# Running the MLP tiles of one batch between the attention heads of the next, with the weights loaded at the start

## The chip, the cores and the metric

One core of a Trainium2 chip runs one launch that computes eight batches of attention and then an MLP over their output. The metric is the device time of a launch in microseconds (us). The time is the median of the runs.

The engines have short names: PE is TensorE, which does matmuls and transposes (PEld is its loading of weights), ACT is ScalarE, DVE VectorE, POOL GpSimd and SP SyncE. Tiles lie in SBUF, the working memory; matmuls write to PSUM, which is dealt out here in eight banks. PEclk is the clock that was granted to PE, as a share of full speed.

## The reference, cut to what matters

```python
def rmsnorm(x, g):
    rms = np.sqrt(np.mean(x * x, axis=-1, keepdims=True) + 1e-06)
    return x / rms * g
# q, k, v: (8 batches, 12 heads, 448, 64) float32
q_n, k_n = rmsnorm(q, g_q), rmsnorm(k, g_k)
attn = softmax(q_n @ k_n.T / sqrt(64))
x = (attn @ v) laid out as (3584 tokens, 768)
h = x @ w_in                     # (768, 2048)
g = 0.5 * h * (1 + tanh(sqrt(2/pi) * (h + 0.044715 * h**3)))
out = g @ w_out                  # (2048, 768), float32
```

The kernels put h * sigmoid(1.702 h) for the gelu. A batch makes 448 tokens; the MLP works in tiles of 512, so tile t needs batches up to (t + 1) * 512 / 448.

## The kernel before

It is two loops, one after the other. The first does a batch at a time: load and square q and k (POOL), sum (DVE), Ln and Exp for the inverse root (ACT), normalise (DVE), transpose on PE; then all 48 score matmuls with their exps, then all 48 PV matmuls; the result goes to a scratch `x` in DRAM.

```python
ps_t = pool("ps_t", bufs=2, PSUM); ps_s = pool("ps_s", bufs=3, PSUM); ps_o = pool("ps_o", bufs=2, PSUM)
for b in range(B):
    qTb = rmsnorm_T(q[b]); kTb = rmsnorm_T(k[b], extra_scale=gqk)
    vaug = vp.tile(...)                       # vp: 2 buffers
    nc.gpsimd.dma_start(vaug[:, :, :, 1:], v[b] ...)
    for h in range(H):
        for sk in range(4):
            scp = ps_s.tile(...); matmul(scp, kT, qT)
            nc.scalar.activation(exs[:, h, sk, :], scp, AF.Exp, scale=scale)
    for h in range(H):
        oap = ps_o.tile(...)                  # 4 PV matmuls accumulate
        osb = copy(oap); otp = transpose(osb) # otp shares ps_t
        xout = otp / its first column
    nc.sync.dma_start(x[b * S:(b + 1) * S, :], xout)
```

Then the attention's pools are closed; the weights are loaded as float32 and cast on ACT; `x` is read back transposed; and the MLP runs seven tiles.

```python
actx.close()
win = load_bf16(moe_w_in); wout = load_bf16(moe_w_out)   # 6 MB DMA each, then a cast on ACT
for c in range(6): nc.sync.dma_start_transpose(xTs[:, c, :], x[:, c * 128:(c + 1) * 128])
for t in range(7):
    for f in range(16):
        hps = ps_h.tile(...)                  # 2 banks; 6 matmuls
        sig = activation(hps, AF.Sigmoid, scale=1.702)
        gsb[:, f, :] = hps * sig
    for (dm0, dmsz) in ((0, 512), (512, 256)):
        for ts in range(4):
            op = ps_m.tile(...)               # 4 banks; 16 matmuls
            osb = copy(op); dma out
```

In the profiles `scp` is a score matmul, `oap` a PV matmul, `otp` the transpose back, `tp` the seven transposes of q or k, `hps` the first and `ops_t` the second MLP matmul.

## Time and profile before

| | before |
|---|---|
| median time | 778.9 us (776.3 to 784.1, 16 runs) |
| span of the profiled run | 776.8 us |
| PE / ACT / DVE / POOL busy | 599.5 / 368.9 / 291.4 / 138.8 us |
| attention, hole, MLP | 373.8, 62.7, 298.8 us |

The windows view of the kernel before, for its attention and the hole after it. The columns are the stretch, its length, then busy time and instruction count of PE, PEld, DVE, ACT and POOL, the granted clock of PE, the DMA share and the GB/s:

```profile
41.50:415.30 373.80, 292.17 (x1763) 163.37 (x1761) 193.39 (x309) 246.88 (x526) 111.78 (x39) 0.90 0.61 73
415.30:478.00 62.70, 6.09 (x12) 1.55 (x13) 0.56 (x1) 23.23 (x5) 0.00 (x0) 0.50 0.95 298
```

By their differences PE is idle for 81.6 us of the attention and 56.6 us of the hole, and for 4 us of the 298.8 us of MLP (busy 294.5). So some 138 us of PE time lie open, while the MLP alone has 294.5 us of PE work that needs only one finished batch to begin. That is what the change goes for.

### The profile page before, as it was taken

The page shows a single profiled execution, that of the slowest core. Times are in us where ns is not written, and L with a number is a line of the kernel's source. Part 1 is how long each engine was busy: PE and PEld are TensorE (multiplying, and loading weights), DVE is VectorE, ACT ScalarE, POOL GpSimd, SP SyncE. Part 2 cuts the span into 40 slices and gives each one's busy share as a digit, 9 for nine tenths or more (in the row PEclk, how much of TensorE's full clock was granted, in tenths as well). Part 3 has the DMA queues.
Part 4 walks back from the last instruction along what each step waited for, and adds up shares of the span by engine and source line. Part 5 has one row for each costly group of instructions (what it writes and reads, how often), then busy time and mean ns, then how long its engine had stood idle before and what let it go on. Part 6 is the DMA issues. An engine that isn't in the chain of part 4 may idle for free.

```text
span 776.8 us, 8528 instructions
## 1 busy us (share of the span) xinstructions
PE 599.5 (77%) x3392; PEld 323.3 (42%) x3392; DVE 291.4 (38%) x435; ACT 368.9 (47%) x705; POOL 138.8 (18%) x54
## 2 busy tenths in 40 slices
PE   0277788787877777877983105999999999999998
PEld 0152644435344353543531001464645445464645
DVE  1843765637456373652612001404041312223140
ACT  1169395582955829468581515324232323323231
POOL 7450631614316053150000000000000000000000
PEclk9879797978999999999997555999999999999999
DMA  6920922909229091390106994020201011010102
GB/s 150 133 72 4 211 72 71 143 1 147 66 82 133 0 165 49 104 40 0 37 1 262 241 370 96 7 75 1 75 7 62 22 41 41 28 54 15 68 1 81
DMA packets 101415, 62.67 MB, mean 81 GB/s; under 512 B 66304, under 2 KB 94976, under 8 KB 100608
## 3 DMA queue, kind: packets, MB, share of 16 engines
q0 software_dynamic: 43136, 5.51, 25.2%
q1 hardware_dynamic: 58240, 56.63, 24.0%
q8 instruction: 26, 0.43, 0.2%
q14 instruction: 13, 0.11, 0.0%
HBM read 45.61 MB, written 16.52 MB: 80 GB/s over the span
## 4 chain that ended last, share of the span: by engine, by line
PE 50%; ACT 23%; POOL 7%; DVE 7%; DMA 5%; SPq 5%; issue 4%; POOLq 0%; ACTq 0%
PE ops_t L192 19%; PE hps L177 18%; ACT exs L118 17%; PE oap L122 8%; POOL sq L72 5%; SPq L163 4%; DVE ss L74 3%; DMA x<-xout 2%; PE otp L130 2%; DMA raw<-in_q_dram 2%; PE tp L87 2%; DVE nrm L81 2%; ACT L78 1%; POOL vaug L104 1%; ACT osb L127 1%
## 5 line engine op out<-in xcount | busy, mean ns | idle before, releaser
L177 PE MATMUL hps<-xTs,dst 128*128 128x512 bf16 x672 | 163.2, 387 | 58.2 <-ACT dst L156 28.1
L118 ACT ACTIVATE exs<-scp 112x448 bf16<-112x448 f32 x384 | 170.7, 669 | 76.5 <-PE scp L115 76.0
L186 DVE TENSOR_TENSOR gsb<-hps,sig 128x512 bf16<-128x512 f32 x112 | 77.4, 692 | 262.8 <-ACT sig L185 262.8
L192 PE MATMUL ops_t<-dst,gsb 128*128 128x256 bf16 (+1 forms) x896 | 154.8, 326 | 0.0
L115 PE MATMUL scp<-xT_sb 128*112 128x448 bf16 x384 | 135.9, 366 | 24.4 <-ACT exs L118 2.3
L177 PEld LDWEIGHTS <-dst 128*128 128x128 bf16 x672 | 66.1, 99 | 145.2 <-issue 47.3
L87 PE MATMUL tp<-ident,nrm 128*128 128x128 bf16 x672 | 63.7, 249 | 65.3 <-DVE nrm L81 34.6
L192 PEld LDWEIGHTS <-gsb 128*128 128x128 bf16 x896 | 87.7, 98 | 59.6 <-DVE gsb L186 1.1
L185 ACT ACTIVATE sig<-hps 128x512 bf16<-128x512 f32 x112 | 66.8, 597 | 96.3 <-PE hps L177 76.6
L122 PE MATMUL oap<-exs,vaug 112*65 112x448 bf16 x384 | 111.9, 405 | 0.0
L115 PEld LDWEIGHTS <-xT_sb 128*112 128x112 bf16 x384 | 50.5, 135 | 85.3 <-issue 79.9
L87 PEld LDWEIGHTS <-nrm 128*128 128x128 bf16 x672 | 52.5, 113 | 79.1 <-issue 75.3
L72 POOL TENSOR_TENSOR sq<-raw 128x2688 f32<-128x2688 f32 x16 | 82.6, 5164 | 9.2 <-DMA raw<-in_q_dram 9.2
L200 ACT COPY osb<-ops_t 128x512 f32<-128x512 f32 (+1 forms) x56 | 26.8, 479 | 107.1 <-PE ops_t L192 107.1
L127 ACT CAST osb<-oap 65x448 bf16<-65x448 f32 x96 | 50.6, 560 | 43.8 <-PE oap L122 43.8
L74 DVE TENSOR_REDUCE ss<-sq 128x42 f32<-128x2688 f32 x16 | 47.2, 2951 | 61.6 <-POOL sq L72 61.6
L81 DVE TENSOR_TENSOR nrm<-raw,rinv 128x2688 bf16<-128x2688 f32 x16 | 53.0, 3314 | 18.4 <-ACT rinv L78 18.4
L130 PE MATMUL otp<-ident,osb 65*112 65x65 bf16 x384 | 37.8, 225 | 26.0 <-ACT osb L127 24.8
L134 DVE RECIPROCAL recip<-otp 112x4 f32<-112x4 bf16 x96 | 17.5, 182 | 106.0 <-PE otp L130 102.8
L130 PEld LDWEIGHTS <-osb 65*112 65x112 bf16 x384 | 33.7, 143 | 51.9 <-ACT osb L127 40.3
L122 PEld LDWEIGHTS <-vaug 112*65 112x65 bf16 x384 | 42.3, 126 | 28.8 <-issue 14.9
L80 POOL MEMSET nrm<- 128x2688 bf16 x16 | 37.4, 2337 | 52.6 <-PE tp L87 52.6
(21 smaller groups left out, 179.8 us busy)
## 6 DMA issues: line engine op xcount, KB each, us to landing
out_dram<-osb SPq DMA_DIRECT2D x28, 256.0 KB, 2.0
tmp<-in_moe_w_in_dram SPq DMA_DIRECT2D x1, 6144.0 KB, 18.0
tmp<-in_moe_w_out_dram SPq DMA_DIRECT2D x1, 6144.0 KB, 18.0
vaug<-in_v_dram POOLq DMA_DIRECT2D x8, 672.0 KB, 13.8
x<-xout SPq DMA_DIRECT2D x8, 672.0 KB, 4.2
out_dram<-osb SPq DMA_DIRECT2D x28, 128.0 KB, 1.7
raw<-in_q_dram SPq DMA_DIRECT2D x8, 0.2 KB, 9.4
raw<-in_k_dram SPq DMA_DIRECT2D x8, 0.2 KB, 6.9
```

Of the source, the lines that this page charges most:

```text
L72: nc.gpsimd.tensor_mul(sq, raw, raw)
L74: nc.vector.reduce_sum(ss, sq, axis=mybir.AxisListType.X)
L81: nc.vector.tensor_mul(nrm[:, :, :D], raw, rinv.to_broadcast([128, NC, D]))
L87: nc.tensor.transpose(tp[:, t * 128:(t + 1) * 128], nrm[:, g * 7 + t, :], ident)
L115: nc.tensor.matmul(scp, kT[:, sk * ST:(sk + 1) * ST], qT, start=True, stop=True)
L118: nc.scalar.activation(exs[:, h, sk, :], scp, AF.Exp, scale=scale)
L122: nc.tensor.matmul(oap, vaug[:, h, sk, :], exs[:, h, sk, :], start=(sk == 0), stop=(sk == nst - 1))
L130: nc.tensor.transpose(otp[:, si, :D + 1], osb[:, si * ST:(si + 1) * ST], ident[:D + 1, :D + 1])
L177: nc.tensor.matmul(hps, win[:, c, f * 128:(f + 1) * 128], xTs[:, c, t * NT:(t + 1) * NT], start=(c == 0), stop=(c == kc - 1),)
L185: nc.scalar.activation(sig, hps, AF.Sigmoid, scale=1.702)
L186: nc.vector.tensor_mul(gsb[:, f, :], hps, sig)
L192: nc.tensor.matmul(op, gsb[:, f, ts * 128:(ts + 1) * 128], wout[:, f, dm0:dm0 + dmsz], start=(f == 0), stop=(f == nf - 1),)
```

## The change

The intent is that an MLP tile runs as soon as its tokens are there, its matmuls filling PE's gaps in the attention of the next batch. Four things make that possible: both weights come early, cast by the DMA; all pools live to the end, and eight PSUM banks are split anew (`tp`/`otp` 1, `sc` 2, `oap` 2, `hps` 1, `ops` 2); sigmoid becomes tanh (sigmoid(a) is (1 + tanh(a/2))/2), so that gelu and exp need no different tables; and V, `xout` and `sq` shrink, and the exps are kept four tiles at a time instead of a whole batch, so that all fits SBUF. The order on each engine comes from the tool's scheduler, not straight from the text.

```diff
+    def load_weights():
+        nc.gpsimd.dma_start(win, moe_w_in ...)      # bf16 tiles: the DMA casts
+        nc.gpsimd.dma_start(wout, moe_w_out ...)
-    vp bufs=2; outp bufs=8; xp bufs=2
+    vp bufs=1; outp bufs=6; xp bufs=1
-        sq = stp.tile([128, NC, D], F32, tag="sq")
+        sq = stp.tile([128, NC, D], BF16, tag="sq")
-            tp = ps_t.tile(...)                     # 2 buffers
+            tp = psum.tile(..., tag="tp", bufs=1)
...
         for h in range(H):
+            oap = psum.tile([D + 1, S], F32, tag="oap", bufs=2)
             for sk in range(nst):
-                scp = ps_s.tile(...)                # 3 buffers
+                scp = psum.tile(..., tag="sc", bufs=2)
                 ... exp ...
+                nc.tensor.matmul(oap, vaug[:, h, sk, :], ex, ...)
-        (second loop over the heads with the PV matmuls)
...
+    def moe_tile(t):
+        xTt: six dma_start_transpose of x's 512 rows
         for f in range(nf):
-            hps = ps_h.tile([128, NT], F32, tag="h")          # 2 buffers
+            if t >= ntt - 2 and f % 3:
+                hps = psum.tile([128, NT], F32, tag="sc", bufs=2)
+            else:
+                hps = psum.tile([128, NT], F32, tag="hps", bufs=1)
-            nc.scalar.activation(sig, hps, AF.Sigmoid, scale=1.702)
-            nc.vector.tensor_mul(gsb[:, f, :], hps, sig)
+            nc.scalar.activation(sig, hps, AF.Tanh, scale=0.851)
+            nc.vector.scalar_tensor_tensor(gsb[:, f, :], sig, 1.0, hps, op0=ALU.add, op1=ALU.mult)
...
-                nc.scalar.copy(osb[:, :dmsz], op)
+                nc.scalar.mul(osb[:, :dmsz], op, 0.5)
...
+    attn_batch(0)
+    win, wout = load_weights()
+    for b in range(1, B):
+        attn_batch(b)
+        (every moe_tile whose tokens are complete before batch b)
+    (the remaining moe_tiles)
```

## The prediction

> **What bounds the kernel now.** I read the page first (slices and groups), then the chain that ended last, then stretches of the windows view, then the timeline. The kernel is two stages one after the other with a hole between them. The slices show it (40 slices of 19.4 us):
>
> ```profile
> PE   0277788787877777877983105999999999999998
> ACT  1169395582955829468581515324232323323231
> PEclk9879797978999999999997555999999999999999
> ```
>
> PE is at 7 to 8 tenths through the attention (slices 2 to 20), near nothing in three slices, and full to the end. The windows view puts numbers on one steady attention batch, the hole, and the second stage:
>
> ```profile
> core 0: us, PE busy (x) PEld busy (x) DVE busy (x) ACT busy (x) POOL busy (x), PEclk, DMA share, GB/s
> 219.30:267.10 47.80, 36.30 (x228) 20.31 (x228) 25.97 (x40) 30.57 (x67) 17.29 (x6) 0.93 0.77 88
> 416.00:478.00 62.00, 6.09 (x12) 1.55 (x13) 0.56 (x1) 23.23 (x5) 0.00 (x0) 0.50 0.95 299
> 560.00:776.00 216.00, 212.81 (x1144) 111.21 (x1142) 55.35 (x80) 67.69 (x122) 0.00 (x0) 1.00 0.11 39
> ```
>
> A batch takes 47.8 us with no engine full; the hole is 62 us with PE at half clock; the MLP is PE-bound at full clock. The chain of waits shows why a batch is 47.8 and not ACT's 31:
>
> ```profile
> 215.50 0.72 ACT osb L127 x2
> 216.24 1.28 ACT L76
> ...
> 230.53 2.03 POOL vaug L104
> 232.56 2.13 issue
> ...
> 237.01 5.70 POOL sq L72
> 242.73 2.95 DVE ss L74
> 245.69 0.60 DVE xT_sb L93
> 247.11 16.17 ACT exs L118 x37
> ```
>
> The last PV matmul frees a V buffer, POOL refills it and only then squares the next batch, DVE sums it, and the transposes and exps wait behind that in order. In the hole, the timeline has the weight loads and two casts on ACT (`ACT dst` 10.4 us each) and six DMA transposes; all 12.6 MB of weights move only when nothing else runs.
>
> The rows I cost with:
>
> ```profile
> L118 ACT ACTIVATE exs<-scp 112x448 bf16<-112x448 f32 x384 | 170.7, 669 | 76.5 <-PE scp L115 76.0
> L115 PE MATMUL scp<-xT_sb 128*112 128x448 bf16 x384 | 135.9, 366 | 24.4 <-ACT exs L118 2.3
> L186 DVE TENSOR_TENSOR gsb<-hps,sig 128x512 bf16<-128x512 f32 x112 | 77.4, 692 | 262.8 <-ACT sig L185 262.8
> ```
>
> **What the Trainium skill says.** "ScalarE: Activation LUTs", section Table sets: tanh is in the set of exp, sigmoid is in another. So tanh among exps needs no switch, and a sigmoid would. The order of the built program agrees: no table load stands before any tanh. The same page, section What ACT_TABLE_LOAD costs, gives about 1283 ns for a load; the trace has 1283 ns for each of its 23. "VectorE: DVE Perf Modes", section on the perf-mode tiers, has tensor_reduce at one element a cycle for either type, so the bf16 `sq` should not shorten the 2.95 us sum (no run here shows it yet). "TensorE: Matmul & The Clock Gate", section The HAM clock gate: an idle PE drops to half clock. The trace agrees: 0.50 in the hole, 1.00 in dense stretches.
>
> **The change part by part.** The instruction counts on PE are the same before and after (3,392 matmuls); they move. The order of the built program shows: batches 0 and 1 almost alone; tile 0 inside batch 2, tiles 1 to 4 inside batches 3 to 6; tile 5 has its few first matmuls inside batch 7 and nearly all of the rest after it, since most of its `hps` now want the `sc` buffers behind the attention; tile 6 last.
>
> PE's streaming cost, from dense stretches of the timeline and chain: scp and oap 0.19 us, transposes 0.107 (7 in 0.75), otp 0.087 (4 in 0.35), hps 0.216, ops_t 0.216 at 512 columns and 0.109 at 256. Counting the built order from the first score of a batch to that of the next gives PE floors of 31.5 (batch 0), 32.8 (1), 55.8 (2), 71.4 (3), 73.1 (4, 5, 6) and 126.5 us (7 with the tail): 543 us with the start's 6. That is the bound that nothing here can beat; the rest is what stalls in between.
>
> 1. *The hole* (62 us) goes. The weights come by casting DMA from POOL at the start, and each tile's transposes are issued some 50 us before their use in the order. The two casts (20.9 us of ACT) go too.
>
> 2. *Batches 0 and 1 get slower.* The transposes and `otp` share one PSUM buffer instead of two, so seven transposes and their copy no longer overlap: 0.9 (cold PE) + 0.04 + 0.65 + 0.04 = 1.65 us a group. Eight groups, one `ss` (2.95) and one `nrm` (2.95) stand before the first score: 19 us, against 8.6 before. The score buffers fall from 3 to 2 and PV is interleaved: a buffer's loop is exp 0.54, semaphore 0.05, one oap 0.19, score with latency 0.35, 0.04: 1.17 us for two exps, 0.585 each, where 37 exps in 16.17 us were 0.437. Twelve heads with their `osb` copy come to about 2.6 us each, 31 us; two split Ln/Exp pairs cost 2.5 us each (32 table loads against 23), the remaining transposes and DVE waits about 3. So batch 1 is 19 + 31 + 5 + 3 = 58 us against 47.8. Batch 0: first score at about 46 (the q and k copies on one buffer), plus 4 because the V load stands behind the 6 MB weight load on POOL's queue; then 31 + 5 + 6 of late batch-1 loads = 42, to 92.
>
> 3. *Batch 2 with tile 0's first part.* 19 us of transposes, 12 heads at about 3 us with some 60 MLP matmuls in the gaps, 7 of stalls: 62, to 212. Then the middle block, 8 groups of six hps, two ops_t, seven transposes. `hps` has one buffer; the chain before shows its loop directly at each tile's start: 1.31 PE + 0.02 + 0.61 ACT + 0.03 + 0.70 DVE + 0.04 = 2.71 us. The other PE work in it fills 1.18 of the 1.4 us wait. 8 x 2.71 = 21.7, plus one `nrm` on DVE in the way, 2.5: 24, to 236.
>
> 4. *Four steady segments* (batches 3 to 6). Two hps groups and the first scores, 6; 96 ops_t, 14.2 (PE-bound, ACT starves); 23 pairs of exps at 0.76 scp/oap + 0.18 otp + 0.43 MLP = 1.37 us of PE against the 1.17 loop, 31.5; Ln and table loads 2.5, `ss` and order misses 3; middle block 24. Sum 81, against a floor of 73; 4 x 81 = 324, to 560.
>
> 5. *The end.* 20 (tile 4's rest), 12 heads at 2.6 = 31, transition 1, then tiles 5 and 6 alone: 178 hps x 0.216 + 126 x 0.216 + 128 x 0.109 = 79.6, and 3.4 us to the end as before: 135. Total 695 us.
>
> The single V buffer (16.5 us from last oap to landed: 0.3 + 0.4 + 2.05 + 13.8) fits behind the 19 to 24 us of transposes, so I charge nothing. `scalar_tensor_tensor` for `tensor_mul` (one PSUM and one SBUF operand, 692 ns) and the halved output copy I take as equal.
>
> **The rivals.** (a) *PE-bound*: the gaps fill so well that the segments sit at 73 to 75 us and batches 0 and 1 at 48: 646 us. For it: MLP matmuls are independent of exps, and PE runs at clock 1.00 when dense. Against: every engine takes its instructions in a fixed order, and `hps`, `tp` and `otp` have one buffer each. (b) *ACT/DVE latency takes PE's place*: with single buffers each misplaced `ss`, `nrm` or Ln holds DVE or ACT for 3 us and with it PE; two per segment more than I charge, and segments of 90, give 735. For it: the before shows exactly such order misses (62 us of DVE waiting for POOL `sq`). (c) *The weight load starves the start*: 6 MB of casting DMA ahead of V, at the V load's own pace (0.67 MB in 13.8 us) instead of the plain loads' 18 us, would shift all by 20 to 40 us: 715 to 735. Against: rows of 8 KB against V's 256 B. (d) *The attention's losses eat the 62 us hole's gain*: 10 us in each of eight batches would be 80; but from batch 3 on the transposes lie beside MLP work, so it's 3 batches.
>
> **Range and chances.** 695, with (a) below and (b) or (c) above: 650 to 740 eight times in ten. The 2% border is 764; only (b) with (c) reach it. Faster 0.93, within 2% 0.05, slower 0.02.
>
> **What would show it.** Right: no stretch of PE below two tenths after slice 3; ACT `dst` rows gone; exps at 0.58 to 0.6 us each in batches 0 and 1; hps groups 2.7 us apart in the middle block; last two tiles at 42 us each; segments of 78 to 84 us; clock near 1.00 from batch 2 on. Wrong: the first score after 55 us (c); waits of PE for DVE copies or `gsb` over 60 us in the steady segments (b); PE over 95% busy there (a); or an `oap` held by the V load, which I took as hidden.

## The result, and the profile after

The changed kernel takes 682.5 us (median of 8 runs, 680.2 to 686.0) against 778.9 us: the ratio is 0.876, with a 95% interval of 0.874 to 0.878. Ratios here are the mean time of one kernel's runs over that of the other's runs of the same rounds, so not quite the ratio of the medians. The predicted 695 us was 12.5 us too slow; the result lies inside the range of 650 to 740. All outputs are right.

The slices of the changed kernel (40 slices of 17 us each):

```profile
PE   0265838766788799878998799888999799999998
...
ACT  0228846851885249824696256933396246942331
...
PEclk9997968776999999999999999999999999999999
```

The empty slices are gone: past the third, no slice of PE is below three tenths. The clock row shows where PE still idles enough to lose its clock: slices 4 to 10, which is where batches 0 and 1 lie.

The windows view of the changed kernel, cut from the first score of one batch to that of the next (batches 0 to 6), then the rest (columns as above). Batches 0, 1, 4 and 6 are shown; the cuts are 39.8, 102.4, 165.0, 232.9, 310.2, 389.4, 468.5 and 543.9 us:

```profile
39.80:102.40 62.60, 39.88 (x231) 23.15 (x230) 34.70 (x43) 41.32 (x76) 26.04 (x9) 0.82 0.96 141
102.40:165.00 62.60, 43.27 (x237) 24.88 (x236) 26.41 (x40) 35.18 (x69) 17.41 (x6) 0.75 0.67 81
...
310.20:389.40 79.20, 70.60 (x456) 40.16 (x453) 36.44 (x56) 46.72 (x92) 16.36 (x6) 1.00 0.63 83
...
468.50:543.90 75.40, 70.24 (x455) 39.98 (x453) 27.65 (x53) 40.66 (x84) 4.63 (x3) 1.00 0.47 51
```

Batches 0 and 1, nearly without MLP work, take 62.6 us each where the kernel before took 47.8. The segments of batches 4 and 5 are 79 us with PE busy for 70.6 of it: a whole MLP tile and a batch of attention. In the kernel before the two together cost 47.8 and a seventh of 298.8, which is 90.5 us, and the hole besides.

The chain that ended last, of the changed kernel, in the middle block between the heads of batch 2 and those of batch 3 (start, us, what):

```profile
212.58 1.42 PE hps L166 x6
214.02 0.61 ACT sig L171
214.65 0.70 DVE gsb L172
215.39 1.47 PE hps L166 x6
```

Six `hps` matmuls, their tanh, their multiply, and only then the next six: the one `hps` bank makes this a loop of 2.81 to 2.86 us. The transposes of the next batch and two `ops_t` matmuls lie in it.

The groups of the changed kernel that answer to the three shown of before (busy us, mean ns, and idle time before):

```profile
L130 ACT ACTIVATE ex<-scp 112x448 bf16<-112x448 f32 x384 | 191.3, 543 | 54.3 <-PE scp L126 52.6
...
L126 PE MATMUL scp<-xT_sb 128*112 128x448 bf16 x384 | 137.1, 370 | 0.0
L172 DVE SCALAR_TENSOR_TENSOR gsb<-sig,hps 128x512 bf16<-128x512 bf16 x112 | 76.8, 686 | 121.7 <-ACT sig L171 121.6
```

The exps are 543 ns each instead of 669. The difference is no gain in speed: in the kernel before exps stood back to back and their recorded times overlap. The new multiply costs the same as the old one, 686 against 692 ns.

### The profile page after: what moved, and what is told of

Read it like the earlier page. It is cut to its first block, busy times and chain, and to the rows that moved or that the text cites. A ratio compares the mean times of both kernels' runs of the same rounds, so it can differ in the third digit from the quotient of the medians.

```text
span 678.5 us, 8823 instructions
## 1 busy us (share of the span) xinstructions
PE 555.7 (82%) x3392; PEld 314.1 (46%) x3392; DVE 283.4 (42%) x435; ACT 365.8 (54%) x712; POOL 135.9 (20%) x56
## 4 chain that ended last, share of the span: by engine, by line
PE 56%; ACT 17%; DVE 10%; issue 9%; DMA 5%; POOL 4%; SPq 0%; ACTq 0%; POOLq 0%
PE hps L166 19%; PE ops_t L178 18%; ACT ex L130 9%; PE oap L131 8%; PE scp L126 6%; DVE gsb L172 5%; ACT sig L171 4%; DMA vaug<-in_v_dram 4%; PE tp L98 2%; DVE nrm L93 2%; POOL sq L84 2%; PE otp L138 2%; ACT osb L135 2%; ACT L130 1%; DMA raw<-in_q_dram 1%
## 5 line engine op out<-in xcount | busy, mean ns | idle before, releaser
L130 ACT ACTIVATE ex<-scp 112x448 bf16<-112x448 f32 x384 | 191.3, 543 | 54.3 <-PE scp L126 52.6
L166 PE MATMUL hps<-xTt,win 128*128 128x512 bf16 x672 | 178.4, 382 | 33.8 <-DVE gsb L172 29.3
L131 PE MATMUL oap<-ex,vaug 112*65 112x448 bf16 x384 | 138.5, 365 | 32.9 <-ACT ex L130 27.4
L178 PE MATMUL ops_t<-wout,gsb 128*128 128x256 bf16 (+1 forms) x896 | 161.2, 326 | 0.1
L172 DVE SCALAR_TENSOR_TENSOR gsb<-sig,hps 128x512 bf16<-128x512 bf16 x112 | 76.8, 686 | 121.7 <-ACT sig L171 121.6
L166 PEld LDWEIGHTS <-win 128*128 128x128 bf16 x672 | 66.2, 99 | 97.7 <-issue 42.6
L84 POOL TENSOR_TENSOR sq<-raw 128x2688 bf16<-128x2688 f32 x16 | 77.5, 4846 | 99.8 <-DMA raw<-in_q_dram 56.6
L185 ACT ACTIVATE osb<-ops_t 128x512 f32<-128x512 f32 (+1 forms) x56 | 26.9, 491 | 76.8 <-PE ops_t L178 76.8
L104 DVE TENSOR_SCALAR xT_sb<-tp,gqk 128x896 bf16<-128x896 bf16 x48 | 32.7, 682 | 79.6 <-PE tp L98 79.6
L86 DVE TENSOR_REDUCE ss<-sq 128x42 f32<-128x2688 bf16 x16 | 47.2, 2947 | 27.1 <-POOL sq L84 27.1
L93 DVE TENSOR_TENSOR nrm<-raw,rinv 128x2688 bf16<-128x2688 f32 x16 | 47.8, 2989 | 4.6 <-ACT rinv L90 4.6
## 6 DMA issues: line engine op xcount, KB each, us to landing
vaug<-in_v_dram POOLq DMA_DIRECT2D x8, 672.0 KB, 14.1
win<-in_moe_w_in_dram POOLq DMA_DIRECT2D x1, 3072.0 KB, 18.9
wout<-in_moe_w_out_dram POOLq DMA_DIRECT2D x1, 3072.0 KB, 41.1
```

What stands on the lines that cost most here:

```text
L84: nc.gpsimd.tensor_mul(sq, raw, raw)
L86: nc.vector.reduce_sum(ss, sq, axis=mybir.AxisListType.X)
L93: nc.vector.tensor_mul(nrm[:, :, :D], raw, rinv.to_broadcast([128, NC, D]))
L130: nc.scalar.activation(ex, scp, AF.Exp, scale=scale)
L131: nc.tensor.matmul(oap, vaug[:, h, sk, :], ex, start=(sk == 0), stop=(sk == nst - 1))
L166: nc.tensor.matmul(hps, win[:, c, f * 128:(f + 1) * 128], xTt[:, c, :], start=(c == 0), stop=(c == kc - 1),)
```

## The experiments

Each run was timed beside the kernel before on the same chip, and the ratios below are to it; the changed kernel's ratio is 0.876. One profile of each was taken. The changed kernel's own runs spread over 6 us, so differences of a few us between single profiles are read with care and the timed ratios decide.

### 1. Only the early weights, without the interleaving

The kernel before, with the two stages still apart. `w_in` comes by a casting DMA at batch 1, `w_out` by one at the seam; to make room, `sq` is bf16 and `xout` and the output buffers shrink as in the change.

```diff
+    win = moe_c.tile([128, kc, d_ff], BF16, tag="win")   # before the attention's pools
...
+        if b == 1:
+            nc.gpsimd.dma_start(win, moe_w_in.rearrange("(c p) f -> p c f", p=128))
...
-        win = load_bf16(moe_w_in, 128, kc, d_ff)
-        wout = load_bf16(moe_w_out, 128, nf, d_model)
+    wout = wpool.tile([128, nf, d_model], BF16, tag="wout")
+    nc.gpsimd.dma_start(wout, moe_w_out.rearrange("(c p) f -> p c f", p=128))
```

> The kernel before, still one stage after the other, with w_in loaded early by a casting DMA and w_out cast on the way at the seam (sq in bf16, one xout buffer and six osb buffers make the room). My theory, that the change gains from both the hole and the overlap of the stages: the two casts and the weight waits leave the hole, about 30 us of it stay (x store 4.2, six transposes of 3.95 each in a row), so about 745 to 750 us, and the other 65 us or so of the change are the interleaving. Rival, that the weight loads are the whole gain and interleaving only pays back what it costs: 685 to 700 us. Rival, that the hole is held by the x store and the transposes: 770 or more.

It took 743.9 us, ratio 0.9555 (0.9523 to 0.9587): about 35 us less than before. The timeline of this run at the seam shows what is left of the hole:

```profile
418.72 24.06 SPq L161 DMA_TRANSPOSE xTs<-x  x6
...
425.40 1.01 PE L175 MATMUL hps<-xTs,win 128*128 128x512 bf16 x2 [11.44 <-DMA xTs<-x]
```

After the store of `x` there are six transposing loads of 24 us, and PE's first MLP matmuls wait for them. So the weights explain about 35 us of the 96 gained, and the other 61 come with the interleaving. Not all of these need matmuls of one stage among those of the other: at this seam PE is still idle for 26.8 us between 413.96 and 446.83 us, and reading `x` back a batch at a time, with the stages apart, might save most of that. No run tried it.

### 2. Sigmoid instead of tanh in the changed kernel

```diff
-            nc.scalar.activation(sig, hps, AF.Tanh, scale=0.851)
-            nc.vector.scalar_tensor_tensor(gsb[:, f, :], sig, 1.0, hps, op0=ALU.add, op1=ALU.mult)
+            nc.scalar.activation(sig, hps, AF.Sigmoid, scale=1.702)
+            nc.vector.tensor_mul(gsb[:, f, :], hps, sig)
-                nc.scalar.mul(osb[:, :dmsz], op, 0.5)
+                nc.scalar.copy(osb[:, :dmsz], op)
```

> The changed kernel with the sigmoid and the plain product put back, interleaved as it is. The built order has 146 table loads in place of 32. My theory: 114 more loads of 1.28 us, 146 us of ACT, most of them inside the loop of two score buffers in the attention, so 60 to 120 us longer: 740 to 800 us. Rival, that ACT has room (54 percent busy) and hides them: under 700 us.

It took 819.0 us, ratio 1.051 (1.046 to 1.056): slower than the kernel before, and above the range expected. The groups of this run by form:

```profile
L166 PE MATMUL hps<-xTt,win 128*128 128x512 bf16 x672 | 190.9, 410 | 91.1 <-DVE gsb L172 84.4 <-DMA xTt<-x 6.3
...
L130 ACT ACT_TABLE_LOAD x66 | 84.7, 1283 | 1.7 <-PE scp L126 0.6
...
L171 ACT ACT_TABLE_LOAD x59 | 75.7, 1283 | 1.0
```

There are 146 table loads in all where the changed kernel has 32. The 114 more, at 1.283 us, are 146 us of ACT, and ACT's busy time rose by 153 us, from 365.8 to 519.1. Many of the loads stand inside the one-bank `hps` loop (59 directly before a sigmoid), and PE waits 84 us for `gsb` instead of 29. The small edit of the activation is what makes the interleaving pay: without it the interleaved kernel is 5% slower than the kernel before, with it 12% faster.

### 3. A second transpose buffer in batches 0 to 2

Every second group of seven transposes borrows one of the `ops` banks, which stand empty then.

```diff
+            if borrow and g % 2:
+                tp = psum.tile([128, 7 * 128], BF16, tag="ops", bufs=2)
+            else:
-            tp = psum.tile([128, 7 * 128], BF16, tag="tp", bufs=1)
+                tp = psum.tile([128, 7 * 128], BF16, tag="tp", bufs=1)
```

> The changed kernel; in batches 0 to 2, which run nearly without MLP work, every second group of seven transposes borrows a bank of the MLP output's two. My theory, that the single shared transpose bank is what makes those batches slow: a group costs about 0.7 us of copy instead of 1.65 us, some 7 us less ahead of the first score of batches 1 and 2 and 3 less at the start, 660 to 668 us. Rival, that the ss and nrm on VectorE and the late loads set the pace there: 677 to 683 us.

It took 674.0 us, ratio 0.8663 (0.8636 to 0.8691): about 8 us less than the changed kernel, where 14 to 22 were expected. The timeline of PE of the changed kernel before batch 1's first score shows what was to be removed (start, us, matmuls, idle before and its releaser):

```profile
89.98 0.91 PE L98 MATMUL tp<-ident,nrm 128*128 128x128 bf16 x7 [0.72 <-DVE xT_sb L102]
...
102.39 0.95 PE L126 MATMUL scp<-xT_sb 128*112 128x448 bf16 x2
```

And the same with the second buffer, from its chain that ended last:

```profile
86.67 0.31 POOL vaug L118
...
87.29 0.10 POOL vaug L119
...
89.33 4.69 POOL sq L84
...
97.53 2.87 DVE nrm L93
```

Without it a group comes every 1.62 us (89.98, then 91.60 and 93.22). With it 49 transposes, seven groups, ran in 4.6 us. Yet batch 1's first score came at 102.2 us, as before. Now the chain of the single V buffer holds it: last PV, POOL's memset and refill of V, only then POOL's next square (89.33), then sum, normalise (97.53) and the last transposes. So by the chain, what was hidden is the bound once the transposes are out of its way; a run with this edit and two V buffers alone was not made. Batches 1 and 2 were shorter, 56.2 and 65.2 us in place of 62.6 and 67.9; some 3 us of that were given back in the two segments after.

### 4. Without the borrowed score banks at the end

```diff
-            if t >= ntt - 2 and f % 3:
+            if t >= ntt and f % 3:
```

> The changed kernel with one hps bank for all tiles, so the last two tiles do not borrow the score banks. The built order moves 18 hps of tile 5 into batch 7 and leaves 162 behind it. My theory, that one bank makes a loop of 2.7 to 2.9 us a group and the borrowed banks hide it: some 27 groups with 0.6 to 1.4 us of wait each, less the 4 us moved, so 12 to 34 us longer, 695 to 715 us. Rival, that borrowing only pushes tile 5 behind the attention, as the prediction put it: 676 to 680 us.

It took 711.0 us, ratio 0.9134 (0.9101 to 0.9166): the borrowing is worth 28 us. The waits view of this run:

```profile
PE hps L166 <- DVE gsb L172: 53.2, 68, 1.7
```

In the changed kernel the same wait is 29.3 us over 45 times. With one bank, tiles 5 and 6 run the 2.8 us loop without other work to fill it. The prediction had said that the borrowing is what pushes tile 5 behind the attention; the trace of this kernel says no: without it 42 instead of 26 `hps` matmuls lie between the first score and the last PV of batch 7, and 12 of them belong to tile 4 in both. Tile 5 comes late either way.

### 5. Two V buffers

```diff
-    vp = ctx.enter_context(tc.tile_pool(name="vp", bufs=1))
+    vp = ctx.enter_context(tc.tile_pool(name="vp", bufs=2))
```

> The changed kernel with two V buffers in place of one. The built order of PE, VectorE, ScalarE and SyncE stays the same, only POOL's changes. The prediction charged nothing for the single buffer: then 681 to 684 us. Rival: in the changed trace POOL waits 129 us in seven waits for the last PV matmul to refill V, and in e3 the refill of 2 us and the squares behind it end just before VectorE sums them; if that chain sets batches 1 and 2, 3 to 5 us each, so 672 to 677 us.

It took 683.3 us, ratio 0.8774 (0.8750 to 0.8799): nothing. Only POOL's order changed. The prediction charged nothing for the single V buffer, and as long as the transposes are single buffered that is right.

### 6. A third score bank in batches 0 and 1

```diff
+                if b < 2 and (h * nst + sk) % 3 == 2:
+                    scp = psum.tile([ST, S], F32, tag="hps", bufs=1)
+                else:
                     scp = psum.tile([ST, S], F32, tag="sc", bufs=2)
```

> The changed kernel, where every third score tile of batches 0 and 1 takes the hps bank, which lies idle then: three score banks as before. My theory: with two banks an exp costs 0.585 us by the loop exp, PV, score; with three it falls towards 0.44 to 0.5, so 48 exps in two batches save 4 to 7 us each, less whatever tile 0's first hps lose: 668 to 674 us. Rival, that the order exp, PV, score on PE, the half clock and the Ln and Exp table loads set the pace and not the number of banks: 680 to 684 us.

It took 682.4 us, ratio 0.8771 (0.8744 to 0.8798): a miss. The heads of both batches did get faster; the last PV of batch 1 ended at 135.1 us, 10.7 earlier than in the changed kernel. But the next dense block of `ops_t` then began at 244.2 us, 6.5 later than there. Batch 2's segment grew from 67.9 to 74.9 us and batch 3's from 77.3 to 84.9. The built order had moved part of tile 0's matmuls from batch 2 to batch 3 (PE is busy there for 76.3 us instead of 69.0), and batch 2 ran at a clock of 0.86 instead of 0.97. I did not isolate what each costs, so the cause of the give-back stays open. What is shown is that the time gained in batch 1 was gone by batch 3.

### 7. Two `hps` banks and one `oap` bank

```diff
-            oap = psum.tile([D + 1, S], F32, tag="oap", bufs=2)
+            oap = psum.tile([D + 1, S], F32, tag="oap", bufs=1)
-                hps = psum.tile([128, NT], F32, tag="hps", bufs=1)
+                hps = psum.tile([128, NT], F32, tag="hps", bufs=2)
```

> The changed kernel with two hps banks and one oap bank. My theory of the middle block, a loop of 2.86 us in one bank with 0.58 us of PE idle in each of 8 rounds and five tiles: two banks take this idle away, 20 to 23 us; but with one oap bank each head waits for the copy of the last one, about 0.63 us in each of the 36 heads of batches 0 to 2 that have nothing beside them, 20 us and more, and in the last batch: 675 to 695 us. Rival, that hps is the costlier of the two: under 668 us; that oap is: over 700 us.

It took 670.4 us, ratio 0.8619 (0.8593 to 0.8645): 11 us less than the changed kernel. That is better than the 675 to 695 us that I had expected, though not under the 668 us of the rival. The groups of this run:

```profile
L166 PE MATMUL hps<-xTt,win 128*128 128x512 bf16 x672 | 184.3, 392 | 9.6 <-DMA xTt<-x 8.6
L131 PE MATMUL oap<-ex,vaug 112*65 112x448 bf16 x384 | 132.1, 365 | 25.5 <-ACT ex L130 19.5
```

The idle time before `hps` fell from 33.8 to 9.6 us, and that before `oap`, where one bank should have hurt, fell from 32.9 to 25.5. By the timeline, `hps` groups in the block between two batches now begin 1.7 to 1.9 us apart where no other wait intervenes (396.56, 398.24, 400.13 us), and the heads of batches 0 and 1, with one `oap` bank, take the same time from first score to last PV (45.6 and 43.4 us; 45.8 and 43.4 in the changed kernel). The second bank belongs to the loop of 2.8 us and not to the PV matmuls. The edit also moved the built order: batch 2 now holds 136 `ops_t` instead of 28. So the 11 us are those of the bank and of the order that comes with it, which no run takes apart.

### 8. Experiments 3, 5 and 6 together

> All three together: a second transpose bank in batches 0 to 2, a third score bank in batches 0 and 1, two V buffers. If the losses of the early batches are these three and add up: 674 of e3 less 8 to 12 for the scores and some 4 for V, 657 to 664 us. If one of them only hid another, no more than e3: 670 to 674 us.

The edit is those three diffs. It took 673.7 us, ratio 0.8658 (0.8632 to 0.8684): no better than the second transpose buffer alone. Batches 0 to 2 took 58.5, 47.0 and 67.3 us, 20.3 us less than in the changed kernel. Batch 3 took 86.9 instead of 77.3, the three segments after it 1.0, 1.3 and 1.2 us more, the rest 2.1 more, 15.2 together. So the early gains are real and most of them are given back after, as in experiment 6.

### 9. Experiments 3 and 7 together

> e7's banks (two hps, one oap) and e3's second transpose buffer in batches 0 to 2 together. If each removes its own wait, the savings of 12 and 8.5 us add: 662 us. If the scheduled order gives part back, as where three changes were joined in e8, 666 to 671. Below 660 neither account would explain it.

The edit is those two diffs. It took 665.2 us (661.7 to 666.3), ratio 0.8546 (0.8517 to 0.8574): the fastest kernel, 2.4% below the changed one by the ratios and 14.5% below the kernel before. Two of its windows, batch 2 and all that follows the first score of batch 7:

```profile
160.80:242.10 81.30, 77.48 (x469) 42.23 (x468) 37.10 (x58) 49.47 (x98) 16.86 (x6) 1.00 0.58 80
...
543.60:659.60 116.00, 107.20 (x603) 56.56 (x600) 31.84 (x60) 54.92 (x107) 0.00 (x0) 1.00 0.14 41
```

Batch 2 is longer, but PE is busy for 77.5 of its 81.3 us (56.1 of 67.9 in the changed kernel): more of tile 0 fits in, and all MLP work moves forward by that much. So the end is 116.0 us instead of 134.6. About 6 of the 8 us that the second transpose buffer brought alone came on top of experiment 7.

### 10. V ahead of the weights

The weight tiles are first touched by two small ACT copies from the V tile, so that their loads wait for V.

```diff
+        nc.scalar.copy(win[:ST, 0, 0:1], vfirst[0][:, 0, 0, 1:2])
+        nc.scalar.copy(wout[:ST, 0, 0:1], vfirst[0][:, 0, 0, 1:2])
         nc.gpsimd.dma_start(win, moe_w_in ...)
```

> Only the first V load is moved ahead of the weight loads on POOL's queue (the weight tiles are touched from the V tile first, so their loads wait for V). The changed kernel's first oap waited 3.24 us for V. If this wait is what the first batch lost, 679 us (3 us less). If the weights now come so late that tile 0 or the start is held, or if the wait only hid another, within 1 us of the changed kernel, 682.

It took 682.9 us, ratio 0.8793 (0.8765 to 0.8821): nothing gained. Its chain at the start:

```profile
15.05 11.03 DMA vaug<-in_v_dram
...
29.62 2.96 DVE nrm L95
```

V landed in 11.0 us and PE no longer waited for it. But the first score came at 42.0 us instead of 39.8. The edit had side effects: the two copies stood on ACT until V had landed, with the Ln of k behind them, and DVE made only one copy of q's transposes before k's normalise at 29.62 us (four in the changed kernel), so that the rest came in a row after it, 1.6 us each. So the run shows that removing the wait in this way gains nothing; it does not show what an edit that leaves ACT free would bring.

### 11. Experiment 9 with V ahead of the weights

> e9 with V ahead of the weights as in e10. If the start's 3 us are real and nothing gives them back, 3 us less than e9; else the same as e9.

It took 667.4 us, ratio 0.8575 (0.8547 to 0.8602), against 0.8546: no gain either, if anything a loss.

### 12. Dummy matmuls to keep the clock up in batches 0 and 1

```diff
+            if warm:                       # batches 0 and 1, after each seven transposes
+                wm = psum.tile([128, NT], F32, tag="hps", bufs=1)
+                for _ in range(3):
+                    nc.tensor.matmul(wm, ident, nrm[:, g * 7:g * 7 + 4, :], start=True, stop=True)
```

> The changed kernel with three dummy matmuls (128x512, into the idle hps bank, never read) after each seven transposes of batches 0 and 1, to keep PE busy while the copy runs. The granted clock in the stretches 39.8 to 102.4 and 102.4 to 165 us was 0.82 and 0.75. If the half clock is what made these batches longer than 58 us, the clock rises to 0.9 or more and each gets some 3 to 4 us shorter: 675. If the latency of the single buffers sets them and the clock only shows the idling, the clock rises and the time stays within 2 us, 681 to 684; if the dummies themselves are in the way (0.65 us each group at full clock, beside a copy of 0.6), up to 690.

It took 687.5 us, ratio 0.8838 (0.8815 to 0.8861), some 6 us slower than the changed kernel. By its windows, the clock rose only from 0.82 to 0.88 between 39.8 and 102.4 us and stayed at 0.75 between 102.4 and 165. The scheduler had put the dummies of batch 1 ahead of its heads, among those of batch 0: the second stretch has no more matmuls than in the changed kernel, 236 against 237. The first score came 3 us later, at 42.8 us. So the test failed to make its condition: it speaks neither for nor against the clock as a cause, it only shows that this way of warming costs more than it brings.

## Why the prediction was right

The mechanism was the predicted one: the hole goes, three early batches pay, and single-buffered loops keep the steady segments a few us above PE's floor. The time was right within 2%. By its own steps, from the profiled run of 678.5 us:

| step | predicted | measured |
|---|---|---|
| 2. first score | 46 | 39.8 |
| 2. batch 0, first score to first score of batch 1 | 65 | 62.6 |
| 2. batch 1 | 58 | 62.6 |
| 3. batch 2 with the middle block | 67 | 67.9 |
| 4. four steady segments | 324 | 77.3 + 79.2 + 79.1 + 75.4 = 311.0 |
| 5. the end | 135 | 134.6 |
| sum | 695 | 678.5 |

(Predicted values are the differences of its milestones 46, 111, 169, 236, 560 and 695 us.)

**Step 1, the hole.** Right: it is gone. Experiment 1 splits the gain: the weights are about 35 us of it. The rest is the read back of `x`, which now happens a tile at a time beside other work, and the gaps of the attention; the record does not divide it between these two.

**Step 2, the start.** The wait of the first PV for V is there, and 3.24 us long where 4 was charged. The timeline of PE has it:

```profile
43.95 0.56 PE L131 MATMUL oap<-ex,vaug 112*65 112x448 bf16 x1 [3.24 <-DMA vaug<-in_v_dram]
```

V took 24.3 us to land behind the first weight load, against a median of 14.1. That is rival (c) in its mildest form. (The 20 to 40 us of that rival do not follow from its own rate: at 0.67 MB in 13.8 us, 6 MB would take over 120 us.) The first score came 6.2 us early since I had charged all of q's and k's transposes on one buffer in a row, and four groups of q's were done before k's normalise. Experiment 10 shows that those 3.24 us are not to be had just by taking the wait away.

**Step 2, batches 0 and 1.** The single buffer cost what was predicted per group at half clock, 1.62 against 1.65 us (whose four terms add up to 1.63). Batch 1 came out 4.6 us over, nearly all of it in its heads: from first score to last PV it took 43.4 us where 39 were charged, and from there to the next first score 19.2 where 19 were. Two terms were too small: at full clock a head took 2.6 to 2.9 us and not 2.6, and the heads were costed at full clock, where the clock granted over those 43.4 us was 0.83. The timeline of ACT in batch 1 of the changed kernel shows a burst at full clock, one Ln and its two table loads, and exps just after:

```profile
111.88 0.98 ACT L130 ACTIVATE ex<-scp 112x448 bf16<-112x448 f32 x2 [0.26 <-PE scp L126]
...
120.48 1.28 ACT L88 ACT_TABLE_LOAD   x1
121.78 0.33 ACT L88 ACTIVATE lg<-ss,eps 128x42 f32<-128x42 f32 x1
122.13 1.28 ACT L130 ACT_TABLE_LOAD   x1
...
128.23 0.54 ACT L130 ACTIVATE ex<-scp 112x448 bf16<-112x448 f32 x1 [0.20 <-PE scp L126]
```

At full clock two exps and their wait come round in 1.23 us (the next pair begins at 113.11), 0.615 each where 0.585 was predicted. The Ln holds the exps for 3.0 us and PE for 2.0. After that the exps come 0.75 us apart (129.08, 129.83), each waiting 0.2 us for its score. PE's own records agree: its PV matmuls take 0.53 us or more from 124.0 us on, and 0.35 again from 130.6. So a stall of 2.0 us was followed by 6.5 us at half clock. The second Ln of this batch, with its loads from 135.85 us, does it again: PE waits 2.77 us up to 139.38 us, and its PV matmuls take 0.53 us or more from 140.8 to 144.1. That the half clock explains most of the excess is an argument from one trace; experiment 12, meant to prove it, did not.

**Step 3, the middle block.** The loop was predicted at 2.71 us and is 2.81 to 2.86; the one `nrm` in the way was there, of 2.87 us, but it cost some 1.1 us (a round of 4.0 us) where 2.5 were charged. Experiments 4 and 7 show from both sides that the one `hps` bank sets it: more tiles on one bank cost 28 us, a second bank gains 11 and its groups come 1.7 to 1.9 us apart.

**Step 4, the steady segments.** They were charged 81 us each and came out 3.7, 1.8, 1.9 and 5.6 under. By PE's timeline the one from 310.2 us divides into 7.9 us of opening, 13.9 of dense `ops_t`, 33.9 of heads (to the last PV) and 23.5 of middle block, where the prediction had 6, 14.2, 37 (31.5 + 2.5 + 3) and 24: the opening was charged 1.9 us too little, the heads with their Ln 3.1 too much, the middle block 0.5 too much. So the 79 us are in part two errors that cancel. The floor of 73 was too high: the prediction took 0.107 us for a transpose from stretches of half clock. At full clock seven take 0.55 us, the first with its latency, so they follow each other by 0.055, and for the 84 of a segment that takes 4.4 us off the floor. PE was busy for 70.6 us. It did not spoil the sum, since most transposes lie in the middle block, where PE waits anyway.

The first of the four was shorter at its opening (4.7 us to its dense block instead of 7.9): the floor that the prediction counted for it was 71.4 and not 73.1, but the sum took it as equal. In the last, batch 8 does not exist: no square, no sum and no Ln fall into it, and one normalise instead of two (POOL 4.6 us, where the others have 16.4). The windows view of the changed kernel has the heads of batch 4 and of batch 6:

```profile
332.00:365.90 33.90, 30.77 (x185) 16.93 (x183) 16.95 (x31) 30.52 (x63) 7.00 (x2) 1.00 0.16 47
490.30:519.90 29.60, 29.40 (x181) 16.45 (x179) 13.40 (x29) 27.01 (x58) 2.34 (x1) 1.00 0.02 7
```

What the last segment lacks it lacks there: PE has 1.4 us less work, and its idle time falls from 3.1 to 0.2 us. Its middle block is no shorter, 24.0 us against 23.5. The step that failed is the multiplication by four.

**Step 5.** Right, 134.6 for 135, and by its parts: 51.0 us from the first score to the last PV of batch 7 where 20 and 31 were charged, 83.6 after it where 84 were. But the words about tile 5 and the borrowed banks in the part on the order were wrong, as experiment 4 showed.

**What was charged nothing.** The bf16 `sq` did not shorten the sum, 2947 against 2951 ns, as predicted. It buys SBUF space: with a float32 `sq` the kernel does not build, since its last SBUF pool asks for 12 KB a partition and 9.3 are left (a build, not a run). The single V buffer is free as the kernel stands (experiment 5) and by the chain of experiment 3 ceases to be once the transposes are double buffered.

So the errors were −6.2, −2.4, +4.6, +0.9, −13.0 and −0.4 us, which makes −16.5. The mis-sizings that matter are the heads of the steady segments, above all of the last, and the start; against them stood the heads and the clock of batch 1. Rival (a), PE-bound, was further off: it had 646 us (its parts, with the other steps as predicted, give 636 to 644), and PE idles for 123 us of the span.

## What to carry to other kernels

When two stages are interleaved, cost the loop of each single-buffered PSUM bank (matmuls, activation, multiply, semaphores) before anything else, and give the spare bank to the longest loop that has nothing to fill it; here one bank moved from `oap` to `hps` was worth 11 us, with the order that it brought, and one lent to the transposes 6 more. Check that the activations of both stages share a table set, since two sets in turn made a gain of 12% a loss of 5%. And do not add up gains of early stages: in two experiments here most of what the first batches gained was given back by the later ones.

## What the Trainium skill lacked or had wrong

- "TensorE: Matmul & The Clock Gate", section PE-mode transpose, gives about 275 ns for a 128x128 bf16 transpose in a kernel and says that full clock does not engage for transposes. In the steady segments, at clock 1.00, each of the 84 was recorded at 217 to 219 ns and seven took 0.55 us, against 0.91 us for seven at half clock. So transposes do run at full clock once it is granted, and packed without gaps they hold it and win it back: in the kernel before, 56 in a row from 278.67 to 283.70 us all took 216 to 230 ns; in experiment 8, after 1.5 us of idle PE, the first 38 of 49 in a row from 137.59 us took 289 to 314 ns and those from 141.69 us on 219, with nothing else on PE between. With gaps they lose it: in the ramp of batch 1, busy for 0.55 of every 1.27 us, after two groups. The same page, in its section The HAM clock gate, has about 3.4 us of idling before the clock drops and about 3.4 us of work to get it back; in batch 1 a wait of 2.0 us was enough, after stretches with smaller waits, and half clock lasted 6.5 us with PE at work in most of it.
- "ScalarE: Activation LUTs", section What ACT_TABLE_LOAD costs, adds a drain of some 1380 ns to the load of 1283 ns for every switch. Here a load took 1283 ns and the Ln began 1.30 us after the load had begun (120.48 and 121.78 us); the exp before it had ended at 120.46. No drain of that size shows.
- No page that I found gives the rate of a casting load. The 6 MB of float32 of `w_in` landed as 3 MB of bf16 in 18.9 us, as fast as the plain 6 MB load of the kernel before (18.0 us); `w_out`, queued behind V, in 41.1 us, and V itself went from 14.1 to 24.3 us.
